# Attention with windows, then soft mixture of experts: the left-over keys in natural order, dispatch weights held still, combine weights divided before use

## The chip, the cores and the metric

The kernel runs on one core of a Trainium2 chip. The metric is the device time of one execution in microseconds. The kernel before took 180.86 us, the median of three runs between 180.55 and 181.25.

A core has a tensor engine (PE, with its weight loads shown as PEld), a vector engine (DVE), a scalar engine (ACT), a general engine (POOL, whose queue starts nearly all transfers here) and a queue for synchronization (SP). Sixteen DMA engines move data between the chip's main memory and the on-chip memory. PE writes into a small accumulator memory (PSUM), from which DVE or ACT copy results out.

## What is computed

Attention runs over 8 batches, 8 heads, 576 positions and 64 channels. The first four heads see a plain window of 32 keys, the last four a dilated one: 32 keys, 4 apart. The result, with heads side by side, is a matrix `x` of 4608 rows and 512 columns, and goes into a soft mixture of 8 experts with 4 slots each:

```
rel = pos[:, None] - pos[None, :]
plain   = (rel >= 0) & (rel < 32)                      # heads 0 to 3
dilated = (rel >= 0) & (rel < 128) & (rel % 4 == 0)    # heads 4 to 7
x = softmax(mask(q k^T / 8)) v                         # 4608 x 512
logits = x @ phi                                       # 4608 x 32 slots
d = softmax of logits over the 4608 rows               # dispatch
slot_input = d^T @ x                                   # 32 x 512
h = relu(slot_input[e] @ w1[e]); slot_out[e] = h @ w2[e]   # F = 1024
c = softmax of logits over the 32 slots                # combine
out = c @ slot_out                                     # 4608 x 512, fp32
```

Inputs are fp32: q, k and v of 9.4 MB each, `w1` and `w2` of 16.8 MB each. The output has 9.4 MB.

## The kernel before

**Transfers.** POOL's queue loads everything but a small table of constants, and converts fp32 to fp16 on the way in and fp16 to fp32 on the way out. It runs in the order of the program. For each batch it loads q, k and v in two parts each (`load_raw`, line 191) into double-buffered tiles, as soon as the tile before has been read. From the fourth batch on, one expert's `w1` follows each v. The rest of `w1` and `w2` follow the last v. The `w2` of experts 5, 6 and 7 come as column halves (line 211): first all first halves, then all second halves. A transfer takes one of eight completion slots, so each waits for the one eight places earlier.

**Attention.** A list of step names (`ORDER`, line 48) fixes by hand the order in which every engine gets its work; each name carries a stage from 0 to 3, so that four batches are in the air at once. In a batch:

- DVE turns q, k and v (`turn`, line 222).
- PE makes scores for groups of key blocks (`emit_scores`, line 263): "P" are five plain blocks of 128 keys, "D" the four dilated residue classes of the first 512 positions, and "L" the last 64 positions of the dilated heads.
- ACT takes the exponentials (line 272), DVE multiplies by 0/1 masks (line 283).
- PE transposes value rows into `vX`, which ACT copies (`v_rows`, `v_place`, lines 237 and 243). Each value row carries an added 1, so that the product also gives the softmax sum.
- PE multiplies probabilities by values (`emit_av`, line 313); DVE takes reciprocals of the sums (line 325); ACT or DVE scale the result into `xp` (plain) or `xd` (dilated) (lines 337 and 341).

For "L", the before kernel handles the 64 left queries by residue class: one score block for the 64 last keys, in which the queries are sorted by class, and 16 more query columns in each "D" block. The product with values is then made in 32 small pieces, each with 16 or 32 rows of result.

**Slots.** For each batch PE transposes x, forms logits (`back_logits`), and ACT takes their exponentials into `ET` (line 408), which stays in memory for all batches with the slots along partitions. `back_erow` and `back_erd` make versions with the rows along partitions. `back_u` (line 451) sums `d^T x` without division: there x is the operand that is held still in PE, and `ET`'s 32 columns stream, in 25 products per batch, 5 of them with a block of ones for the sums. DVE adds the batch's part to `UT` (line 461).

**The end.** After the last batch, PE sums `ET` over slots into `rs` (lines 585 and 590). DVE takes the reciprocals `rcol` (line 593) and `rrow` (line 607), and scales the slot inputs (line 599). PE multiplies by `w1` (`hps`, line 616), ACT and DVE apply the ReLU (lines 623 and 624), PE transposes (line 626), DVE and ACT copy (lines 628 and 631), and PE multiplies by `w2` (`so`, line 646), in two column halves. Four partial sums on partition groups are joined: copied to `so_part` (line 660), added by a product with `spread` (line 665), and copied to `so_sb` (line 666). Then for each block of 128 output rows PE multiplies `ET` by `so_sb` (line 672), and ACT or DVE in turn scale by `rrow` while copying to `om` (lines 681 and 685). POOL's queue stores it (line 692): six batches by column halves, two whole, and the left rows (line 721).

Of the kernel before, what the change touches and what calls it, by code (L numbers as in the profile page):

```python
# [32 lines left out]
NV = 10  # L33
# [3 lines left out]
DW = 144  # L37
LEFT = SUB - 128
# [6 lines left out]
    (("P", 3), ("P", 4), ("L", 0), ("D", 0)),  # L45
# [12 lines left out]
WIDTH = {"P": PW, "L": DIL * LEFT, "D": DW}  # L58


def piece_w(kind, i):
    return S - 512 if (kind, i) == ("P", 4) else WIDTH[kind]

# [15 lines left out]
def make_consts():  # L79

    a = np.arange(128)[:, None]
    rel = np.arange(PW)[None, :] - a
    band = (rel >= 0) & (rel < WINDOW)
    one = np.ones((1, N_SLOTS), bool)
    r, i = np.divmod(np.arange(DIL * LEFT)[None, :], LEFT)
    parts = [band, (a < 64) & (a % DIL == r) & (a // DIL <= i)]
    parts.append(((a % 32) < LEFT) & one)
    parts.append((a < 64) & one)
    parts.append(a == np.arange(128)[None, :])
    parts.append((a % 32) == (np.arange(128)[None, :] % 32))  # L90
    parts.append((a // 32) == np.arange(4)[None, :])
    return np.ascontiguousarray(np.concatenate(parts, axis=1).astype(np.float16))
# [3 lines left out]
def kernel(  # L96
# [18 lines left out]
    band, lmask = cst[:, 0:PW], cst[:, PW : PW + DIL * LEFT]  # L115
    o_em = PW + DIL * LEFT
    o = o_em + 2 * N_SLOTS
    ident = cst[:, o : o + 128]
    spread = cst[:, o + 128 : o + 256]
    quad = cst[:, o + 256 : o + 260]  # L120
    masks = consts.tile([128, NMASK], FP16, name="masks")
    emask = consts.tile([128, 6, N_SLOTS], FP16, name="emask")
    phi_raw = consts.tile([128, 4, N_SLOTS], FP16, name="phi_raw")
    phi4 = consts.tile([128, 4, 4, N_SLOTS], FP16, name="phi4")
    ones = consts.tile([128, 128], FP16, name="ones")
    ET = consts.tile([128, 192 * B], FP16, name="ET")
    UT = consts.tile([128, 5, N_SLOTS], FP32, name="UT")
    rcol = consts.tile([128, N_SLOTS], FP32, name="rcol")
    siTm = consts.tile([128, 4, E_EXP, N_SLOTS], FP16, name="siTm")
    rrow = consts.tile([128, NFIN], FP32, name="rrow")  # L130
# [25 lines left out]
    x_pool = tc.alloc_tile_pool(name="xp", bufs=2)  # L156
# [5 lines left out]
    ring = ctx.enter_context(tc.tile_pool(name="ring", bufs=2, space=bass.MemoryType.PSUM))  # L162
# [6 lines left out]
    def build_masks():  # L169
# [8 lines left out]
        for kind, i in GROUPS[1]:  # L178
            w = piece_w(kind, i)
            copies(o, lmask if kind == "L" else band, w, 1)  # L180
            o += w
        nc.scalar.copy(
            out=emask[:, 4:6, :], in_=cst[:, o_em : o_em + 2 * N_SLOTS].rearrange("p (t s) -> p t s", t=2)
        )
# [39 lines left out]
    V_PARTS = ((0, 1, 2), (3, 4), (5, 6, 7), (8, 9))  # L224

    def v_rows(b, part):
        tiles = V_PARTS[part]
        rg = ring.tile([128, len(tiles), 4, 2, 32], FP16, name=f"rv_{b}_{part}", tag="ring")
        for n_t, t in enumerate(tiles):
            for c in range(2):  # L230
# [4 lines left out]
                else:  # L235
                    rows = vT[:, 1, 512:SK, c]
# [10 lines left out]
    def emit_scores(b, g):  # L247
        kb, qb = kT[b % 2], qT[b % 2]
        sps = psum_s.tile([128, 4, 512], FP32, name=f"s_{b}_{g}", tag="s")
        for kind, i in GROUPS[g]:  # L250
            c0, w = PIECE[(kind, i)][1], piece_w(kind, i)
            for tt in range(2):
                for h in range(4):
# [5 lines left out]
                    elif kind == "D":  # L259
                        kk, qq = kt[:, i:512:DIL], qt[:, i:S:DIL]  # L260
                    else:
                        kk, qq = kt[:, 512:SK], qt[:, 512:S].rearrange("p (i r) -> p r i", r=DIL)
# [11 lines left out]
    def emit_mask(b, g):  # L274
# [4 lines left out]
        else:  # L279
            m = masks[:, 0 : GW[0]].rearrange("p (n w) -> p n w", n=3)[:, :, 0:DW]  # L280
            m = m[:, None, :, :].broadcast_to([128, 4, 3, DW])
# [8 lines left out]
    xp_t, xd_t = {}, {}  # L290

    def emit_av(b, kind, i):
        o = psum_o.tile([128, 4, D + 1], FP32, name=f"o_{b}_{kind}{i}", tag="o")
        jobs, vb = [], vX[b % 2]
        for h in range(4):
            if kind == "L":
                for r in range(DIL):
                    p = probs(b, "L", 0, h, LEFT * r, 32)[0:64]
                    jobs.append((slice(32 * r, 32 * r + 32), p, vb[0:64, 9, h, 0 : D + 1], h))
# [3 lines left out]
        for h in range(4):  # L303
# [3 lines left out]
            elif kind == "L":  # L307
                for r in range(DIL):
                    lhs = probs(b, "D", r, h, 128, LEFT)
                    rows = slice(32 * r, 32 * r + LEFT)  # L310
                    jobs.append((rows, lhs, vb[:, NP + r, h, 0 : D + 1], h))
        for n, (rows, lhs, rhs, h) in enumerate(jobs):
# [4 lines left out]
                start=(n == 0 or (kind == "L" and n < DIL)),  # L317
# [10 lines left out]
    def norm_mult(b, kind, i, o, rc, engine):  # L328
        pool, name = (xp_t, "xp") if kind == "P" else (xd_t, "xd")
        if b not in pool:  # L330
            pool[b] = x_pool.tile([128, 5, 4 * D], FP16, name=f"{name}_{b}", tag=name)
        dst = pool[b][:, 4 if kind == "L" else i, :]
# [18 lines left out]
    def x_half(b, kind, t, c):  # L351
        return (xp_t if kind == "P" else xd_t)[b][:, t, 128 * c : 128 * c + 128]
# [7 lines left out]
    def xT_dil(b, c):  # L360
# [3 lines left out]
        nc.tensor.transpose(rg[:, :, 128:160], x_half(b, "D", DIL, c), ident)  # L364
# [45 lines left out]
    def back_erow(b):  # L410
        m, l = et_cols(b)
        ep = ring.tile([128, 6, N_SLOTS], FP16, name=f"ep_{b}", tag="ring")
        left = ET[0:32, l : l + 128]
# [3 lines left out]
        nc.tensor.transpose(ep[:, 5, :], left, ident[0:32, 0:32])  # L417
        for r in range(DIL):
            nc.tensor.transpose(
                ep[32 * r : 32 * r + 32, 4, :],  # L420
                left.rearrange("p (i r) -> p r i", r=DIL)[:, r, :],
                ident[0:32, 0:32],
            )
        return ep

    def back_er(b, ep):
        er = s_pool.tile([128, 6, N_SLOTS], FP16, name=f"er_{b}", tag="er")
        nc.vector.tensor_tensor(out=er, in0=ep, in1=emask, op=ALU.mult)
# [8 lines left out]
    def back_u(b):  # L437
        up = ring.tile([128, 5, N_SLOTS], FP32, name=f"u_{b}", tag="ring")
        er, erd = er_t.pop(b), erd_t.pop(b)
        jobs = []  # L440
        for t in range(NP):
            e = er[:, t if t < 4 else 5, :]
            for c in range(2):
                jobs.append((c, x_half(b, "P", t, c), e))
            jobs.append((4, ones, e))
        for r in range(DIL + 1):
            e = erd[:, r, :] if r < DIL else er[:, 4, :]
            for c in range(2):
                jobs.append((2 + c, x_half(b, "D", r, c), e))
# [310 lines left out]
```

## Time and profile before

| what | value |
|---|---|
| median of the runs | 180.86 us |
| the profiled execution | 180.9 us, of which 178.9 us are its span |
| busy: PE, DVE, ACT, POOL | 128.0, 125.7, 122.2, 56.2 us |
| PE instructions: products, and weight loads | 2316, 2316 |
| read from main memory, written | 62.07 MB, 9.44 MB |

The span is the time from the first to the last instruction on the core. The profile has a row of forty slices of the span, with the DMA engines' mean share and the data rate of each; groups of equal instructions with their summed busy time and mean duration; timelines; and for each stretch of time the busy time of each engine, the clock granted to PE, the DMA share and the rate. The rate counts bytes as written, so an fp32 load into fp16 is read at twice the rate shown.

### The profile page before, as it was taken

To read this page: it belongs to the slowest core of one execution; us is meant where nothing else is said; L and a number is where in the kernel's file an instruction comes from. 1 tells how busy PE (TensorE), PEld (TensorE's weight loads), DVE (VectorE), ACT (ScalarE), POOL (GpSimd) and SP (SyncE) were. 2 spreads that over 40 slices of the span, in tenths; PEclk is the share of its full clock that TensorE was granted. 3 is DMA by queue.
4 is the path that set the end of the run, shared out by engine and by line. 5 is a ranking of instruction groups with operands and counts; after the bars stand their busy time and mean duration, and the time that the engine had idled before them with its cause. 6 is when DMAs were issued, how large, how long until landed. Compare 5 with 4: busy or idle time off the path is not lost.

```text
span 178.9 us, 5405 instructions
## 1 busy us (share of the span) xinstructions
PE 128.0 (72%) x2316; PEld 84.7 (47%) x2316; DVE 125.7 (70%) x274; ACT 122.2 (68%) x267; POOL 56.2 (31%) x94
## 2 busy tenths in 40 slices
PE   0026838989999999989989999988695346688100
PEld 0014525676667767657767757856434112221000
DVE  6483999999999999999999995472402016789200
ACT  6007757999999999999999999966002016698100
POOL 7544244224224223243420041111112414376400
PEclk9999999999999879999999999687669955555555
DMA  5999999999999999999999999999999999999994
GB/s 91 203 213 208 214 212 210 214 212 216 214 212 213 215 212 215 214 212 216 210 214 215 212 218 220 215 216 220 211 212 191 197 196 219 390 319 397 406 413 135
DMA packets 21448, 40.88 MB, mean 229 GB/s; under 512 B 1713, under 2 KB 14129, under 8 KB 20785
## 3 DMA queue, kind: packets, MB, share of 16 engines
q0 software_dynamic: 21280, 40.41, 114.2%
q8 instruction: 18, 0.29, 0.6%
q1 hardware_dynamic: 144, 0.14, 0.3%
q14 instruction: 6, 0.04, 0.1%
HBM read 62.07 MB, written 9.44 MB: 400 GB/s over the span
## 4 chain that ended last, share of the span: by engine, by line
DMA 52%; DVE 16%; PE 11%; ACT 9%; issue 3%; POOL 2%; POOLq 0%; DVEq 0%
DMA w<-in_moe_w_dram 36%; DMA rawV<-in_v_dram 10%; DMA rawK<-in_k_dram 6%; DVE vT L222 5%; DVE qk L222 4%; DVE p L283 3%; PE f L672 3%; ACT p L272 3%; ACT om L681 2%; PE s L263 2%; PE o_P L313 2%; PE rv L237 2%; ACT xp L337 1%; PE rp L357 1%; ACT vX L243 1%
## 5 line engine op out<-in xcount | busy, mean ns | idle before, releaser
L272 ACT ACTIVATE p<-s 128x1728 f16<-128x1728 f32 (+1 forms) x24 | 42.0, 1749 | 10.7 <-PE s L263 10.6
L263 PE MATMUL s<-qk 32*128 32x144 f16 (+2 forms) x640 | 29.2, 325 | 16.1 <-DVE qk L222 12.3
L313 PEld LDWEIGHTS <-p 128*128 128x128 f16 (+3 forms) x672 | 23.9, 101 | 14.0 <-issue 3.6
L263 PEld LDWEIGHTS <-qk 32*128 32x128 f16 x640 | 17.0, 118 | 20.4 <-DVE qk L222 12.3
L337 ACT ACTIVATE xp<-o_P,rc_P 128x64 f16<-128x64 f32 x96 | 23.8, 384 | 2.4 <-DVE rc_P L325 2.3
L283 DVE TENSOR_TENSOR p<-p,masks 128x1728 f16<-128x1728 f16 (+1 forms) x24 | 25.4, 1082 | 0.0
L243 ACT COPY vX<-rv 128x512 f16<-128x512 f16 (+1 forms) x32 | 23.5, 786 | 1.7 <-PE rv L237 1.6
L313 PE MATMUL o_P<-vX,p 128*128 128x65 f16 (+1 forms) x288 | 20.7, 210 | 1.3 <-DVE xp L341 0.3
L222 DVE STREAM_TRANSPOSE qk<-rawQ 128x576 uint32<-128x576 uint32 x16 | 18.9, 1243 | 2.7 <-DMA rawQ<-in_q_dram 2.7
L222 DVE STREAM_TRANSPOSE qk<-rawK 128x576 uint32<-128x576 uint32 x16 | 19.7, 1241 | 0.5 <-DMA rawK<-in_k_dram 0.5
L222 DVE STREAM_TRANSPOSE vT<-rawV 128x576 uint32<-128x576 uint32 x16 | 19.6, 1238 | 0.4 <-DMA rawV<-in_v_dram 0.4
L237 PE MATMUL rv<-cst,vT 128*128 128x128 f16 x160 | 17.3, 248 | 3.0 <-DVE vT L222 1.7
L211 POOL DMA_DIRECT2D w<-in_moe_w_dram x12 | 8.9, 745 | 29.1 <-DMA w<-in_moe_w_dram 24.8
L685 DVE TENSOR_SCALAR om<-f,rrow 128x256 f16<-128x256 f32 (+1 forms) x28 | 13.5, 518 | 3.9 <-PE f L672 3.1
L237 PEld LDWEIGHTS <-vT 128*128 128x128 f16 x160 | 12.0, 127 | 8.6 <-issue 4.3
L191 POOL DMA_DIRECT2D rawQ<-in_q_dram x16 | 8.9, 557 | 21.5 <-DVE rc_P L325 16.3
L681 ACT ACTIVATE om<-f,rrow 128x256 f16<-128x256 f32 (+1 forms) x28 | 12.8, 503 | 3.3 <-PE f L672 2.6
L672 PE MATMUL f<-so_sb,ET 32*128 32x256 f16 (+1 forms) x60 | 12.1, 420 | 3.7 <-ACT om L681 2.4
L692 POOL DMA_DIRECT2D out_dram<-om x14 | 10.4, 747 | 12.1 <-DVE om L685 9.4
L191 POOL DMA_DIRECT2D rawK<-in_k_dram x16 | 8.7, 548 | 17.1 <-DVE rc_P L325 14.6
L191 POOL DMA_DIRECT2D rawV<-in_v_dram x16 | 8.7, 547 | 10.8 <-DVE rc_P L325 8.0
L372 ACT COPY xT<-rp 128x576 f16<-128x576 f16 x16 | 10.5, 776 | 1.2 <-PE rp L357 1.2
(84 smaller groups left out, 197.4 us busy)
## 6 DMA issues: line engine op xcount, KB each, us to landing
w<-in_moe_w_dram POOLq DMA_DIRECT2D x13, 1024.0 KB, 21.7
out_dram<-om POOLq DMA_DIRECT2D x12, 512.0 KB, 6.2
rawQ<-in_q_dram POOLq DMA_DIRECT2D x16, 288.0 KB, 10.7
rawK<-in_k_dram POOLq DMA_DIRECT2D x16, 288.0 KB, 10.4
rawV<-in_v_dram POOLq DMA_DIRECT2D x16, 288.0 KB, 10.2
w<-in_moe_w_dram POOLq DMA_DIRECT2D x12, 256.0 KB, 16.4
out_dram<-om POOLq DMA_DIRECT2D x2, 1024.0 KB, 8.6
out_dram<-om_l POOLq DMA_DIRECT2D x2, 512.0 KB, 9.1
```

The costliest lines, as they stand in the source:

```text
L191: nc.gpsimd.dma_start(out=t[g::2, :], in_=src[4 * g : 4 * g + 4].rearrange("h (p j) d -> (h p) (j d)", j=PJ),)
L222: nc.vector.transpose(out=out_, in_=in_)
L237: nc.tensor.transpose(rg[:, n_t, :, c, :], rows, ident)
L243: copy(out=vX[b % 2][:, t0 : t0 + n, :, 0:D], in_=rg.rearrange("p n h c d -> p n h (c d)"))
L263: nc.tensor.matmul(sps[:, h, c0 : c0 + w], kk, qq, start=(tt == 0), stop=(tt == 1))
L272: return nc.scalar.activation(out=pt, in_=sps[:, :, 0:n], func=AF.Exp, scale=SCALE)
L283: return nc.vector.tensor_tensor(out=pt, in0=pt, in1=m, op=ALU.mult)
L313: nc.tensor.matmul(o[rows, h, :], lhs, rhs, start=(n == 0 or (kind == "L" and n < DIL)), stop=(n == len(jobs) - 1), skip_group_check=True,)
L337: nc.scalar.activation(out=dst[:, h], in_=src[:, h], func=AF.Copy, scale=rc[:, h : h + 1])
L672: nc.tensor.matmul(fp[:, 0 : c1 - c0], ET[32 * j : 32 * j + 32, m : m + 128], so_sb[32 * j : 32 * j + 32, c0:c1], start=True, stop=True,)
L681: nc.scalar.activation(out=dst, in_=fp[:, 0 : c1 - c0], func=AF.Copy, scale=rrow[:, blk : blk + 1])
L685: nc.vector.tensor_scalar(out=dst, in0=fp[:, 0 : c1 - c0], scalar1=rrow[:, blk : blk + 1], scalar2=None, op0=ALU.mult)
```

## The change

Four things change.

1. The 64 left queries of the dilated heads stay in natural order. There are now two "L" score blocks, each with 128 neighbouring keys, from 448 and from 384 on, with a mask of their own; the "D" blocks lose their 16 extra columns. The product with values takes two products of 128 keys for each head instead of eight small ones. A value tile is added (11 instead of 10).
2. In `back_u` the row version of `ET` is held still and x streams, with a column of ones stored beside x. The 25 products become 10, and the sum has the slots along partitions. At the end it is scaled, transposed back by PE and copied into `siTm`.
3. The combine weights are divided in place: for each pair of batches PE sums `ET` over the slots with a block matrix, DVE takes the reciprocal of 128x384 elements and multiplies. Two such divisions stand before the products with `w1`, two between their halves. `rrow` disappears.
4. Output blocks are copied two at a time, without scaling, by ACT and DVE in turn. The first products with `w2` take 512 columns, and the joins of `so` are made in one copy per half, the second one wholly before the sixth batch's output.

```
-NV = 10
+NV = 11
-DW = 144
-LEFT = SUB - 128
+LEFT = S - 512
+XW = 4 * D + 2
...
-    (("P", 3), ("P", 4), ("L", 0), ("D", 0)),
+    (("P", 3), ("P", 4), ("L", 0), ("L", 1), ("D", 0)),
...
+LKEY = (448, 384)
...
-    V_PARTS = ((0, 1, 2), (3, 4), (5, 6, 7), (8, 9))
+    V_PARTS = ((0, 1, 2), (3, 4), (5, 6, 7), (8, 9, 10))
...
                     elif kind == "D":
-                        kk, qq = kt[:, i:512:DIL], qt[:, i:S:DIL]
+                        kk, qq = kt[:, i:512:DIL], qt[:, i:512:DIL]
                     else:
-                        kk, qq = kt[:, 512:SK], qt[:, 512:S].rearrange("p (i r) -> p r i", r=DIL)
+                        kk, qq = kt[:, LKEY[i] : LKEY[i] + 128], qt[:, 512:S]
...
             if kind == "L":
-                for r in range(DIL):
-                    p = probs(b, "L", 0, h, LEFT * r, 32)[0:64]
-                    jobs.append((slice(32 * r, 32 * r + 32), p, vb[0:64, 9, h, 0 : D + 1], h))
+                for n in range(2):
+                    lhs = probs(b, "L", n, h, 0, 128)
+                    jobs.append((slice(0, 128), lhs, vb[:, NP + DIL + n, h, 0 : D + 1], h))
...
     def back_u(b):
-        up = ring.tile([128, 5, N_SLOTS], FP32, name=f"u_{b}", tag="ring")
+        up = ring.tile([64, 4 * D + 1], FP32, name=f"u_{b}", tag="ring")
         er, erd = er_t.pop(b), erd_t.pop(b)
...
+            n = LEFT if t == 4 else 128
+            for k, x in enumerate((xp_t[b % 2], xd_t[b % 2])):
+                e = erd[:, t, :] if k == 1 and t < 4 else er[0:n, t, :]
+                nc.tensor.matmul(
+                    up[32 * k : 32 * k + 32, :],
+                    e,
+                    x[0:n, t, 0 : 4 * D + 1],
+                    start=(t == 0),
+                    stop=(t == NP - 1),
+                )
...
+    nc.vector.reciprocal(out=rcol, in_=U[:, 4 * D : 4 * D + 1])
+    nc.vector.tensor_scalar(out=si, in0=U[:, 0 : 4 * D], scalar1=rcol, scalar2=None, op0=ALU.mult)
+    siT = ring.tile([128, 2, 2, N_SLOTS], FP16, name="siT", tag="ring")
+    for c in range(2):
+        nc.tensor.transpose(
+            siT[:, c].rearrange("p k s -> p (k s)"), si[:, 128 * c : 128 * c + 128], ident[0:64, 0:64]
+        )
...
+    def normalize(pr):
+        cols = ET[:, 384 * pr : 384 * pr + 384]
+        rs = ring.tile([128, 384], FP32, name=f"rs_{pr}", tag="ring")
+        rr = h_pool.tile([128, 384], FP32, name=f"rr_{pr}", tag=f"rr{pr % 2}")
+        nc.tensor.matmul(rs, block, cols, start=True, stop=True)
+        nc.vector.reciprocal(out=rr, in_=rs)
+        nc.vector.tensor_tensor(out=cols, in0=cols, in1=rr, op=ALU.mult)
+
+    for pr in range(2):
+        normalize(pr)
...
     for fc in range(2):
+        if fc == 1:
+            for pr in range(2, 4):
+                normalize(pr)
         for g in range(2):
...
+    psum_f = tc.alloc_tile_pool(name="psum_f", bufs=3, space=bass.MemoryType.PSUM)
...
+    def join_so(s):
+        cols = slice(DH * s, DH * s + DH)
+        nc.vector.tensor_copy(out=so_part[:, cols], in_=so[:, cols])
+        nc.tensor.matmul(rep[:, cols], spread, so_part[:, cols], start=True, stop=True)
+        nc.scalar.copy(out=so_sb[:, cols], in_=rep[:, cols])
+
+    def emit_fin(blocks, c0, c1, dst, name, copy):
+        fp = psum_f.tile([128, 2, DMODEL], FP32, name=f"f_{name}_{c0}", tag="f")
+        for n, (m, j) in enumerate(blocks):
...
+        copy(out=dst, in_=fp[:, :, 0 : c1 - c0])
...
+    EVICT = (nc.scalar.copy, nc.vector.tensor_copy)
...
-    for s in range(2):
-        emit_so(s, (0, 1, 2, 3))
-    for s in range(2):
-        emit_so(s, (4,))
+    emit_so(None, (0, 1, 2, 3))
+    emit_so(None, (4,))
     for e in (5, 6, 7):
         emit_so(0, (e,))
-    gather_so(0)
-    spread_so(0)
+    join_so(0)
     for b in range(NHALF):
         if b in (2, 3, 5):
             emit_so(1, ({2: 5, 3: 6, 5: 7}[b],))
         if b == 5:
-            gather_so(1)
+            join_so(1)
         emit_batch(b, 0, DH)
-    spread_so(1)
```

## The prediction

> **What bounds the kernel now.** I read the page first, then the table of stretches over the end, the timelines of VectorE, ScalarE and the POOL queue, and last the groups with shapes kept apart. From the page:
>
> ```profile
> span 178.9 us, 5405 instructions
> ...
> DMA  5999999999999999999999999999999999999994
> GB/s 91 203 213 208 214 212 210 214 212 216 214 212 213 215 212 215 214 212 216 210 214 215 212 218 220 215 216 220 211 212 191 197 196 219 390 319 397 406 413 135
> ...
> q8 instruction: 18, 0.29, 0.6%
> ```
>
> The DMA engines never rest: fp32 inputs come in at some 213 GB/s of fp16 written (twice that read), and the fp32 result leaves at 400. VectorE, ScalarE and TensorE are busy too, but only the transfers are busy from end to end. So compute matters where it decides when a transfer can start, and that is at one place: the first output store. From the table of stretches (after the stretch: busy time and count of PE, PEld, DVE, ACT, POOL, then PE clock, DMA share, GB/s):
>
> ```profile
> 146.00:150.00 4.00, 2.69 (x26) 0.94 (x22) 2.33 (x6) 2.21 (x6) 0.69 (x1) 0.50 1.45 195
> 150.00:151.00 1.00, 0.45 (x12) 0.14 (x8) 0.88 (x2) 0.84 (x2) 0.81 (x2) 0.50 1.22 186
> ...
> 157.00:159.00 2.00, 1.71 (x9) 0.48 (x9) 1.55 (x4) 1.83 (x5) 1.39 (x2) 0.50 1.08 214
> 159.00:176.00 17.00, 6.16 (x23) 1.14 (x20) 7.24 (x13) 6.33 (x12) 6.57 (x10) 0.50 1.73 401
> ```
>
> The stores replace the last loads almost without a hole (only 150 to 151 and 157 to 159 sag). From the POOL timeline, the last load and the first and sixth store:
>
> ```profile
> 143.36 0.74 POOL L211 DMA_DIRECT2D w<-in_moe_w_dram  x1 [1.44 <-DMA w<-in_moe_w_dram]
> ...
> 149.31 0.75 POOL L692 DMA_DIRECT2D out_dram<-om  x1 [5.21 <-DVE om L685]
> ...
> 157.61 2.96 POOL L692 DMA_DIRECT2D out_dram<-om  x4 [2.73 <-DVE om L685]
> ```
>
> Each transfer marks its landing 16 times in the trace, once per DMA engine. The last load's marks run from 150.10 to 153.58 us, so the engines are up to 3.5 us apart. The trace's 18 instruction packets (16 KB each, 18 for PE's 4632 instructions, one per 257) explain this: half of the 16 marks trail, and after the packets at 22.1, 80.6 and 140.7 us the latest mark falls 0.7 to 0.9 us further back. The latest engine has three. It is busy from 153.58 to the last mark, 177.39; the span ends 1.5 us later. Sixth store to last, 12 half-batches take 15.5 us between first marks: 1.29 us each. A store reaching idle engines lands 3.0 us after its issue (149.31 to 152.31, 157.61 to 160.62), so its data start after 1.7.
>
> Two rates for the change, from the timelines of ScalarE and VectorE and the groups:
>
> ```profile
> 95.95 1.61 ACT L243 COPY vX<-rv 128x768 f16<-128x768 f16 x2
> 97.32 1.07 ACT L337 ACTIVATE xd<-o_D,rc_D 128x64 f16<-128x64 f32 x4
> ...
> 98.91 0.79 ACT L243 COPY vX<-rv 128x512 f16<-128x512 f16 x1
> 99.37 1.83 ACT L272 ACTIVATE p<-s 128x1728 f16<-128x1728 f32 x1
> ```
> ```profile
> 79.10 0.16 DVE L325 RECIPROCAL rc_D<-o_D 128x4 f32<-128x4 f32 x1
> 79.14 0.15 DVE L325 RECIPROCAL rc_P<-o_P 128x4 f32<-128x4 f32 x1
> ...
> 127.43 0.32 DVE L461 TENSOR_TENSOR UT<-UT,u 128x160 f32<-128x160 f32 x1 [0.92 <-PE u L451]
> ...
> 128.38 0.37 DVE L607 RECIPROCAL rrow<-rs 128x36 f32<-128x36 f32 x1
> 135.06 0.69 DVE L624 TENSOR_SCALAR h_sb<-hps 128x512 f16<-128x512 f32 x1 [6.30 <-ACT h_sb L623]
> ```
> ```profile
> L685 DVE TENSOR_SCALAR om<-f,rrow 128x256 f16<-128x256 f32 x24 | 10.6, 480 | 3.6 <-PE f L672 3.0
> ...
> L325 DVE RECIPROCAL rc_P<-o_P 128x4 f32<-128x4 f32 x40 | 6.1, 168 | 2.9 <-PE o_P L313 2.6
> ...
> L685 DVE TENSOR_SCALAR om<-f,rrow 128x512 f16<-128x512 f32 x4 | 2.9, 748 | 0.3 <-PE f L672 0.2
> ...
> L607 DVE RECIPROCAL rrow<-rs 128x36 f32<-128x36 f32 x1 | 0.4, 374 | 0.0
> ```
>
> ScalarE runs back to back in the attention: start to start, a 768-wide value copy takes 0.69 us and a 512-wide one 0.46. From 4 to 36 elements a reciprocal grows by (374-168)/32 = 6.4 ns an element, where an eviction of VectorE grows by (748-480)/256 = 1.05.
>
> **The change part by part**, along the chain that leads to the first store. It starts at 127.75, the end of the last UT sum.
>
> A. Attention. The exponentials and masks keep their sum (1920+1920+1536 columns for 1920+1728+1728). TensorE loses some 33 small products a batch net and gains two value transposes; that is worth nothing, because ScalarE sets the pace, and could only cost if TensorE (4.6 of 5 us busy) became the slower one, which less work excludes. The fourth value copy grows from 512 to 768: 0.21 us in each of 8 batches on the engine that never waits, 1.7 us; ScalarE pauses some 0.3 us a batch, and the first batch is not full. I take +1.3 (ends 0 and 1.7). The loads do not notice: POOL keeps 4 to 7 transfers in flight here.
>
> B. Dispatch sums. 25 products of 32 columns (0.82 us for the last batch) become 10 of 257, two at a time on separate output strips. At the half clock four 512-column products of hps (L616) run together: their weight loads come in fours, 0.43 us apart. So a 257-column pair takes 0.21: 5 pairs and a tail, 1.3 us, less four small transposes. With 257 instead of 160 elements to add: +0.45 (ends 0; 1.5 if pairs don't overlap).
>
> C. To the first wide reciprocal: reciprocal 0.17, slot scaling 0.39, two transposes 0.35, the product with `block` 0.45: 1.35 us.
>
> D. The four divisions of `ET` now stand on VectorE ahead of the ReLU of line 624 that today starts at 135.06. Each is a reciprocal of 384 elements, 168+380x6.4 = 2.6 us, and a 384-wide product at about 0.5 (0.40 for 256, row L341): 4x3.1 = 12.4. Ends: at a copy's rate 4x1.07 = 4.3; at the 10 ns an element that the starts 79.10 and 79.14 allow, 4x4.4 = 17.6, though that interval may be a floor for short instructions. I trust the difference of durations. Today's pause of VectorE (6.3 us before L624) hides half of it; the ReLU moves to 143.2. Behind the divisions on VectorE stand that ReLU, the copy of `hT`, and `so_part`, and for these wait TensorE, ScalarE and POOL. On TensorE the last two `block` products wait for buffers of the first two reciprocals and hold up the second half of hps to some 138 us; the divisions are still later, so that is free.
>
> E. ReLU to the first `so` product: 137.03-135.06 = 1.97 us, unchanged.
>
> F. `so`, first half: today its products wait for loads until 145.6. Now all are there, and 10 groups of 512 columns (both halves of experts 0 to 4) and 6 of 256 come in a row: at the half clock, which PE will have after its pause, 10x0.43+6x0.21 = 5.6 us; at full clock 2.8. I take 5.3.
>
> G. `so` to the first store's issue: 149.31-146.04 = 3.3 us. Wider join copies cost 0.1 each, the pairwise eviction (128x512: 0.69 and 0.75 us) gains as much. POOL's list of transfers is the same, and nothing but stores queues behind this wait; SP has the constants alone.
>
> Sum: 127.75+1.3+0.45+1.35+12.4+1.97+5.3+3.3 = 153.8 us, 4.5 later than now. From an idle start the span ends 1.7+18x1.29+0.3+1.5 = 26.7 us after the first issue: 180.5, against 178.9. The break-even is a first issue at 152.2.
>
> Later on nothing adds: evictions at 0.75 us a half-batch, POOL's issue (0.75) and the join of the second half (some 1.5 us, with four stores queued) keep up with 1.29. The reserved gain is hidden: PE's 4010 instructions need 15 blocks instead of 18, so no engine has three; that is worth 0.7 to 0.8 us only if the stores are ready when the loads end. Constants (32 KB more), memsets and smaller copies lie beside the first loads, cost 0 to 0.1.
>
> The profiled execution took 180.9 us, 2.0 beyond its span, and the median of the runs is 180.86. So 180.9+1.6 = 182.5 us.
>
> [...]
>
> **Rivals.**
> 1. Reciprocals cost midway between durations and start-to-start interval, 8.2 ns an element: 3.3 us each, D is 15.4, the time 185.5. For it speaks 79.10 to 79.14; against it the durations. [...]
> 2. Not slower: the wide reciprocal streams better than short ones. If D falls to 4.3, the first store could go at 145.7; the loads then decide, and the missing third block gives 180.9-0.8 = 180.1. Below D = 10.8 us the change costs nothing, below 9.8 the loads decide. Against it: nothing in the trace shows a reciprocal at that rate.
> 3. In between: D as said, but `so` at full clock (-2.5) or no delay from A (-1.3): first issue 151.3 to 152.5, time 180.1 to 181.2. For it: hps brought the clock up 4.4 us after its start at 128.5.
> 4. The change doesn't reduce what bounds: certain for the products, since ScalarE paces attention and DMA the whole.
>
> **How the numbers follow.** A measurement here tells 0.5%, 0.9 us. Forecast (181.8 to 184.0, own range) 0.46; rival 1 and longer 0.14; rivals 2 and 3 in the band 180.0 to 181.7, 0.27; below it 0.13, where rival 2 meets a further lost stall, such as the 157 to 159 sag. So 0.13 faster, 0.27 same, 0.60 slower. The range reaches from the floor of rival 2 to rival 1: 180.0 to 185.3.
>
> **What would show it.** Wide reciprocals of 2.6 us; the ReLU near 143; the first store near 153.8 with DMA share falling towards zero between 151 and 155; 15 instruction packets; no landing spread of 3.5 us. I am wrong if the ReLU starts before 140, or if the stores have further holes.

## The result and the profile after

The changed kernel takes 182.14 us (median of 22 runs, 180.68 to 183.93), the kernel before 181.04 us (22 runs beside them, 180.55 to 181.66). The ratio is 1.0053, with a 95% interval from 1.0038 to 1.0069: slower by half a per cent. A run more than 1.5% above the fastest of its kernel (183.93 here, and one such run below) stays out of the ratios. The profiled execution took 182.9 us, 1.8 more than its span; for the kernel before the distance was 2.0.

From the page of the changed kernel:

```profile
span 181.1 us, 4758 instructions
...
DMA  5999999999999999999999999999999997999997
GB/s 112 172 205 210 211 212 213 213 213 216 210 213 214 215 213 214 211 214 213 212 214 215 213 215 223 217 213 212 221 203 193 196 196 101 271 394 399 402 412 208
...
q8 instruction: 15, 0.25, 0.5%
```

There are 15 instruction packets where there were 18. Slice 34 sags to 101 GB/s, and the first two slices are at 112 and 172 GB/s, before at 91 and 203. The table of stretches shows the hole (the columns are those of the table of before: busy time of PE, PEld, DVE, ACT, POOL, then PE clock, DMA share, GB/s):

```profile
146.00:150.00 4.00, 3.48 (x38) 1.31 (x40) 0.42 (x1) 0.58 (x1) 0.00 (x0) 0.54 1.45 196
150.00:151.00 1.00, 1.00 (x36) 0.61 (x24) 0.00 (x0) 0.00 (x0) 0.00 (x0) 1.00 1.13 161
151.00:153.50 2.50, 0.90 (x17) 0.39 (x9) 1.08 (x2) 1.09 (x3) 0.00 (x0) 1.00 0.56 73
153.50:155.80 2.30, 2.06 (x34) 0.84 (x37) 1.88 (x4) 1.87 (x4) 1.57 (x3) 1.00 0.29 61
155.80:157.00 1.20, 0.38 (x9) 0.10 (x4) 1.06 (x3) 0.18 (x1) 1.20 (x2) 0.80 1.99 404
```

For almost five microseconds the transfers have next to nothing to do: from 151.0 to 155.8 the rate is 73 and then 61 GB/s, while `so`, which TensorE ended at 151.15, is joined and the first output blocks are made. Stores run only from 155.8. VectorE, the groups with shapes kept apart, and the POOL timeline say why:

```profile
130.31 0.41 DVE L443 TENSOR_TENSOR U<-U,u 64x257 f32<-64x257 f32 x1 [1.33 <-PE u L429]
...
132.11 2.56 DVE L583 RECIPROCAL rr<-rs 128x384 f32<-128x384 f32 x1 [0.24 <-PE rs L582]
134.70 0.56 DVE L584 TENSOR_TENSOR ET<-ET,rr 128x384 f16<-128x384 f16 x1
...
143.88 0.56 DVE L584 TENSOR_TENSOR ET<-ET,rr 128x384 f16<-128x384 f16 x1
144.36 0.68 DVE L608 TENSOR_SCALAR h_sb<-hps 128x512 f16<-128x512 f32 x1
146.21 0.42 DVE L612 COPY hTm<-hT 128x512 f16<-128x512 f16 x1 [1.17 <-PE hT L610]
```
```profile
L583 DVE RECIPROCAL rr<-rs 128x384 f32<-128x384 f32 x4 | 10.2, 2552 | 0.2 <-PE rs L582 0.2
...
L584 DVE TENSOR_TENSOR ET<-ET,rr 128x384 f16<-128x384 f16 x4 | 2.2, 558 | 0.1
```
```profile
154.10 3.84 POOL L671 DMA_DIRECT2D out_dram<-om  x5 [10.25 <-ACT om L658]
160.71 2.96 POOL L671 DMA_DIRECT2D out_dram<-om  x4 [2.77 <-DVE om L658]
```

The four divisions fill VectorE from 132.11 to 144.36 without a pause, the ReLU stands behind them, and POOL waits 10.25 us for the first block of output, where it waited 5.21. The first store goes at 154.10 instead of 149.31.

Not all of this is the divisions. The attention also starts later, as the first exponential shows, in the kernel before and then in the changed one:

```profile
13.30 1.77 ACT L272 ACTIVATE p<-s 128x1920 f16<-128x1920 f32 x1 [8.95 <-PE s L263]
```
```profile
14.96 1.77 ACT L270 ACTIVATE p<-s 128x1920 f16<-128x1920 f32 x1 [10.48 <-PE s L261]
```

### The profile page after: what moved, and what is told of

Same layout as the page of the kernel before. It is cut to its first block, busy times and chain, and to the rows that moved or that the text cites. A ratio compares the mean times of both kernels' runs of the same rounds, so it can differ in the third digit from the quotient of the medians.

```text
span 181.1 us, 4758 instructions
## 1 busy us (share of the span) xinstructions
PE 119.3 (66%) x2004; PEld 78.3 (43%) x2004; DVE 134.3 (74%) x267; ACT 119.0 (66%) x251; POOL 56.2 (31%) x94
## 4 chain that ended last, share of the span: by engine, by line
DVE 47%; DMA 15%; PE 11%; ACT 11%; issue 5%; POOL 1%; DVEq 1%; POOLq 0%; ACTq 0%
DVE qk L219 12%; DVE p L281 8%; DVE vT L219 8%; DMA rawV<-in_v_dram 6%; DVE rr L583 6%; DMA phi_raw<-in_moe_phi_dram 6%; DMA rawK<-in_k_dram 4%; DVE xd L329 4%; PE so L633 3%; PE f L651 2%; ACT p L270 2%; DVE om L658 2%; ACT xp L325 2%; ACT om L658 2%; ACT xT L366 2%
## 5 line engine op out<-in xcount | busy, mean ns | idle before, releaser
L270 ACT ACTIVATE p<-s 128x1920 f16<-128x1920 f32 (+1 forms) x24 | 44.3, 1847 | 12.1 <-PE s L261 11.9
L261 PE MATMUL s<-qk 32*128 32x128 f16 (+2 forms) x704 | 26.7, 295 | 20.2 <-DVE qk L219 13.9
L241 ACT COPY vX<-rv 128x768 f16<-128x768 f16 (+1 forms) x32 | 27.5, 932 | 1.9 <-PE rv L235 1.9
L304 PEld LDWEIGHTS <-p 128*128 128x128 f16 (+1 forms) x480 | 22.1, 102 | 13.5 <-issue 4.0
L325 ACT ACTIVATE xp<-o_P,rc_P 128x64 f16<-128x64 f32 x96 | 26.3, 490 | 2.2 <-DVE rc_P L316 2.2
L281 DVE TENSOR_TENSOR p<-p,masks 128x1920 f16<-128x1920 f16 (+1 forms) x24 | 25.6, 1082 | 0.1
L235 PEld LDWEIGHTS <-vT 128*128 128x128 f16 x176 | 13.1, 124 | 7.8 <-issue 3.8
L671 POOL DMA_DIRECT2D out_dram<-om x14 | 10.3, 745 | 13.1 <-ACT om L658 10.2
L658 DVE CAST om<-f 128x512 f16<-128x512 f32 (+1 forms) x14 | 10.2, 765 | 3.7 <-PE f L651 3.7
L304 PE MATMUL o_D<-vX,p 128*128 128x65 f16 x128 | 9.9, 202 | 2.3 <-DVE xp L329 1.7
L366 ACT COPY xT<-rd 128x576 f16<-128x576 f16 x16 | 10.6, 790 | 0.2 <-PE rd L352 0.2
```

The source lines that it names most:

```text
L235: nc.tensor.transpose(rg[:, n_t, :, c, :], rows, ident)
L241: copy(out=vX[b % 2][:, t0 : t0 + n, :, 0:D], in_=rg.rearrange("p n h c d -> p n h (c d)"))
L261: nc.tensor.matmul(sps[:, h, c0 : c0 + w], kk, qq, start=(tt == 0), stop=(tt == 1))
L270: return nc.scalar.activation(out=pt, in_=sps[:, :, 0:n], func=AF.Exp, scale=SCALE)
L281: return nc.vector.tensor_tensor(out=pt, in0=pt, in1=m, op=ALU.mult)
L304: nc.tensor.matmul(o[rows, h, :], lhs, rhs, start=(n == 0), stop=(n == len(jobs) - 1), skip_group_check=True,)
```

## The experiments

First the price of the divisions by itself, then its break-even, the parts that pay for some of it, and two causes that fell. What a profile gives of each kernel is gathered at the end of this section.

**Two divisions moved.** The first two divisions stay; the third goes behind the copy of `hT`, the fourth into the second half of the stores.

```
     for pr in range(2):
-        normalize(pr)
+        divide(pr, ring_sums(pr))
     ...
         if fc == 1:
-            for pr in range(2, 4):
-                normalize(pr)
+            rs_2 = ring_sums(2)
     ...
+    divide(2, rs_2)
     ...
         emit_batch(b, DH, DMODEL)
+        if b == 2:
     ...
+            divide(3, sums(3, f3[:, 0, 0:384]))
```

Here `normalize` is split in two: `sums` and `ring_sums` are its product on TensorE, `divide` its reciprocal and product on VectorE.

> The changed kernel with the four divisions kept but two of them moved: the third stands behind the copy of hT, the fourth behind the third half-batch of the second half (nine stores out). Chain theory (the end is the first store's issue plus 27 us as soon as that issue is later than about 152.2; the four divisions, 12.3 us on VectorE ahead of the ReLU, make it late): the ReLU starts about 138.5 instead of 144.4, the first store goes at 148.5 to 150.5, the loads decide again, time 180.0 to 180.6 us, below the kernel before. Rival 'late start' (in the profile of the changed kernel one DMA engine runs 2.3 us behind from the first loads on and the first exponential starts 1.66 us later; that is what costs, the divisions cost nothing net): 182 us, as the changed kernel. Rival 'stores' (the pairwise evictions and the joins make the store phase longer): 182 us too, with 27 us or more after the first store.

Measured: 180.07 us (179.84 to 180.74), ratio to the kernel before 0.9949 (0.9934 to 0.9964). From its VectorE and POOL timelines:

```profile
129.44 2.56 DVE L585 RECIPROCAL rr<-rs 128x384 f32<-128x384 f32 x1
...
136.04 0.69 DVE L612 TENSOR_SCALAR h_sb<-hps 128x512 f16<-128x512 f32 x1 [0.40 <-ACT h_sb L611]
137.54 0.42 DVE L616 COPY hTm<-hT 128x512 f16<-128x512 f16 x1 [0.80 <-PE hT L614]
137.88 2.55 DVE L585 RECIPROCAL rr<-rs 128x384 f32<-128x384 f32 x1
140.46 0.56 DVE L586 TENSOR_TENSOR ET<-ET,rr 128x384 f16<-128x384 f16 x1
145.65 0.42 DVE L649 CAST so_part<-so 128x256 f16<-128x256 f32 x1 [4.63 <-PE so L638]
```
```profile
148.66 0.75 POOL L676 DMA_DIRECT2D out_dram<-om  x1 [5.04 <-ACT om L663]
```

The same reciprocals, the same 2.55 us each, but the ReLU now ends a wait of 0.40 us (put down to ScalarE's half of the ReLU) and not a queue of divisions, and the third division lies in VectorE's wait for `so`, which still leaves 4.63 us. The ReLU starts at 136.04, 2.5 us ahead of the expectation; the first store at 148.66 and the time are inside it. The chain theory holds. The edit leaves the code of the start and of the pairwise evictions as it was, so neither rival expects the gain. This execution did start earlier than the profiled one of the changed kernel (first exponential 13.77 for 14.96); that an early start alone does not make the kernel fast is shown by two runs below, with every reciprocal twice (13.46) and with the divisions in the kernel before (13.22).

**No divisions.**

```
-    for pr in range(2):
-        normalize(pr)
     ...
-            for pr in range(2, 4):
-                normalize(pr)
```

> The changed kernel with the division of the combine weights left out (the sums, the reciprocals and the products; the output is then not divided). Chain theory: the ReLU starts at 137 to 138 (hps decides), loads decide, 180.0 to 180.6 us, the same as with two divisions moved. Late start or stores: 182 us.

Measured: 180.11 us (180.01 to 180.85), ratio 0.9956 (0.9939 to 0.9973). Leaving the divisions out gains no more than moving two of them. The ReLU starts at 136.31, a little ahead of the expectation. At this end the loads decide: the time is the last load's latest mark, 153.91, plus 26.9 us.

**Every reciprocal twice.**

```
         nc.vector.reciprocal(out=rr, in_=rs)
+        nc.vector.reciprocal(out=rr, in_=rs)
```

> The changed kernel with each of the four wide reciprocals issued twice, 4 x 2.55 = 10.2 us more on VectorE. Chain theory: all of it reaches the end, since the first store is already later than the loads: first store 164.3, time 192.3 (191.8 to 192.8). If the divisions were partly hidden in the changed kernel (late start or stores decide), less than 10.2 arrives, by as much as was hidden: 188 to 191.

Measured: 191.12 us (190.24 to 193.54, four runs), ratio 1.0539 (1.0504 to 1.0574), so some 9 of the 10.2 us arrive. The median lies between the ranges of the two; by the ratio the time is 190.8 us, inside that of the rival. The timeline has all the extra time (130.97 to the ReLU at 153.59, 22.6 us where the changed kernel has 12.25, and a first store at 164.30, as expected), but its execution is the one of 193.54 us; the other three took 190.24, 190.28 and 191.95. Why a microsecond or more is missing in them isn't settled.

**One division moved**, the fourth alone:

```
-            rs_2 = ring_sums(2)
+            divide(2, ring_sums(2))
     ...
-    divide(2, rs_2)
```

> The changed kernel with the fourth division alone moved behind nine stores, the other three left ahead of the ReLU: 3.1 us off the chain. Chain theory with its break-even at a first store of 152.2 (so that D costs nothing below 10.8 us and the loads decide below 9.8): D is 9.2 us, first store 150.2 to 151.2, time 180.1 to 180.5 us, all but as good as two divisions moved (180.07). Rival (no sharp break-even, since the 16 DMA engines end their loads 3 us apart, so each us of the chain costs part of itself on the early ones): about halfway between 180.07 and 182.14, 180.8 to 181.3.

Measured: 180.16 us (179.77 to 180.51), ratio 0.9960 (0.9941 to 0.9979). Taking 3.1 us off the chain gains all that there is, 2.0; the further 3.1 of the first experiment gain nothing that can be told from zero. The break-even of the prediction is there, and the rival's gradual price is not. How sharp it is isn't shown: the first store of the profiled execution went before the expected 150.2 to 151.2, some 2 us ahead of the break-even.

```profile
149.28 2.37 POOL L675 DMA_DIRECT2D out_dram<-om  x3 [6.17 <-ACT om L662]
```

**The left block's products five times over**, on top of two divisions moved:

```
-        for n, (rows, lhs, rhs, h) in enumerate(jobs):
+        for _ in range(5 if kind == "L" else 1):
+            for n, (rows, lhs, rhs, h) in enumerate(jobs):
```

> Two divisions moved, and the products of the left block issued five times over (each repetition starts its sums anew, the result is the same): 512 more instructions on TensorE, 4522, so 17 or 18 instruction packets of 16 KB again instead of 15, the 17th before the last loads land as in the kernel before. ScalarE still sets the pace of the attention (the kernel before has more instructions). Packet theory (a third packet on one DMA engine puts it 0.7 to 0.9 us further back, and the latest engine ends the kernel): 180.7 to 181.0 us. Rival (what is gained against the kernel before comes from the evictions in pairs, the joins or what lies outside the span): 180.0 to 180.2 us, as without the repetitions.

Measured: 180.76 us (180.33 to 181.05), ratio 0.9985 (0.9971 to 0.9999), where it was 0.9949 without the repetitions: 0.7 us more. The page has the packets:

```profile
span 179.1 us, 5271 instructions
...
q8 instruction: 17, 0.28, 0.6%
```

In this trace the last load's latest mark falls at 153.89, in the one without repetitions at 153.31, and the first store still goes in time (149.99). The last mark alone would not tell, since the kernel without divisions has one at 153.91 with 15 packets, after a start that was later on one engine. But the step itself can be seen. Here and without repetitions the eighth load's marks spread over 0.97 and 0.99 us, and the last load's first mark falls at 150.17 and 150.14. Only the latest mark moves: around the 17th packet, at 147.9, the spread goes from 3.07 us in one load to 3.94 in the next, where the kernel without repetitions stays at 3.15 to 3.17. So the packet theory stands: with the packets back, most of the gain against the kernel before is gone. About a quarter of a microsecond more of that gain lies outside the span (1.76 us here and with two divisions moved, 2.0 in the kernel before); what it is isn't shown.

One part of the expectation fell: ScalarE does not go on setting the pace. The 32 extra products in each batch, with their weight loads, made a batch of the attention 0.7 us longer (13.58 for 12.86) and the whole attention 5.1 us, and from 55 to 80 us ScalarE is busy for 24.39 of 25 us and VectorE for 23.59, where without them they are for 25.00 and 24.92. This reaches the first store only by 1.3 us, and that is still before the break-even. In the traces of the kernel before and of the changed one the instruction packets have 16384 bytes each (18 beside 2316 products of TensorE and as many weight loads, 15 beside 2004). Here 512 instructions more for TensorE, in 17 packets, cost 0.7 us.

**The divisions in the kernel before**, and nothing else of the change:

```
     nc.vector.reciprocal(out=rrow, in_=rs)
+    nc.tensor.matmul(ds, spread, ET[:, 0:384], start=True, stop=True)
+    for _ in range(4):
+        nc.vector.reciprocal(out=dr, in_=ds)
+        nc.vector.tensor_tensor(out=dt, in0=ET[:, 0:384], in1=dr, op=ALU.mult)
```

> The kernel before with four dummy divisions (reciprocal and product of 128 x 384, result unused) on VectorE where the change has them, and nothing else of the change. Chain theory: VectorE's pause of 6.3 us hides half of the 12.3, the ReLU goes from 135.06 to 141.2, the first half of so then runs in a row on loads that are there, first store 149.5 to 152, break-even 152.2: time 181.0 to 181.6 us. Rival (the division alone explains the changed kernel's time): 182.1 us.

Measured: 183.37 us (181.77 to 184.33), ratio 1.0123 (1.0076 to 1.0169), above both expectations. Its VectorE timeline:

```profile
129.27 0.32 DVE L461 TENSOR_TENSOR UT<-UT,u 128x160 f32<-128x160 f32 x1 [0.91 <-PE u L451]
...
130.52 2.50 DVE L613 RECIPROCAL dr<-ds 128x384 f32<-128x384 f32 x1
...
143.08 0.68 DVE L631 TENSOR_SCALAR h_sb<-hps 128x512 f16<-128x512 f32 x1
```

The divisions take what they should (12.6 us). But the last dispatch sum ends at 129.60, where the profile that the prediction was made from has 127.75: the attention of this execution was longer, from the first exponential to the last transposition of `ET` 114.3 us against 112.4. So the base was 1.85 us too early for this execution, and the first store goes at 153.31, after the expected 149.5 to 152. From there to the end it takes 30.2 us, where the changed kernel takes 28.8. And the divisions alone cost more than the whole change: its other parts give back about 1.2 us, though the four runs lie 2.6 us apart. The difference behind the first store would account for it. One place where the stores differ is the stretch from 160 to 162 us, here and then in the changed kernel:

```profile
160.00:162.00 2.00, 1.71 (x9) 0.40 (x7) 1.56 (x4) 1.83 (x5) 1.50 (x3) 0.50 1.39 278
```
```profile
160.00:162.00 2.00, 1.62 (x12) 0.56 (x12) 1.67 (x4) 1.66 (x3) 1.29 (x2) 0.50 1.97 391
```

Which of the other parts (the evictions in pairs, the joins) does it, no run separates.

**A shorter value copy.** In the changed kernel, step A undone:

```
-        copy(out=vX[b % 2][:, t0 : t0 + n, :, 0:D], in_=rg.rearrange("p n h c d -> p n h (c d)"))
+        n = min(n, NV - 1 - t0)
+        copy(out=vX[b % 2][:, t0 : t0 + n, :, 0:D], in_=rg[:, 0:n].rearrange("p n h c d -> p n h (c d)"))
     ...
+        nc.vector.memset(vX[i][:, NV - 1, :, 0:D], 0.0)
```

> The changed kernel with the fourth value copy of ScalarE 512 wide as before, not 768 (the second key tile of the left block is left zero, so the last 64 queries of the dilated half are wrong). Step A of the prediction: 8 x 0.21 us less on the engine that sets the pace, 1.3 us (0 to 1.7) of it on the chain: last dispatch sum 1.3 us earlier, time 180.6 to 181.0 where the changed kernel has 182.1. Rival (the later end of the attention is the late start alone, ScalarE has pauses that hide the copies): 182.

Measured: 181.04 us (180.35 to 182.88, ten runs), ratio 1.0022 (0.9989 to 1.0055). The median says 1.1 us, but the runs fall into two groups with a hole between: six from 180.35 to 181.26 at a mean granted clock of .882 to .884, and four from 182.48 to 182.88 at .848 to .856. The changed kernel's own runs at .882 to .900 are 180.68 to 180.94, and those at .846 to .857 are 182.49 to 183.28. At like clocks the shorter copy is worth some 0.1 to 0.3 us, though the changed kernel's runs between these clocks (.864 to .877) spread from 181.19 to 183.93. Over four batches in the middle of the attention a batch takes 12.87 us here, 12.91 in the changed kernel, 12.86 in the one without divisions and 12.87 in the kernel before. From the tables of stretches, 55 to 80 us, of the kernel before, the changed one, and this one:

```profile
55.00:80.00 25.00, 23.64 (x501) 17.21 (x485) 24.81 (x56) 24.81 (x55) 7.19 (x13) 0.93 1.06 213
```
```profile
55.00:80.00 25.00, 21.55 (x435) 16.06 (x428) 24.93 (x57) 25.00 (x56) 7.96 (x14) 1.00 1.06 213
```
```profile
55.00:80.00 25.00, 22.86 (x442) 16.36 (x439) 24.94 (x56) 24.99 (x57) 7.57 (x14) 1.00 1.06 213
```

VectorE (third number) is as full as ScalarE (fourth), with the long copy and without. ScalarE alone doesn't set this pace. Over the whole attention the copy does show: in three profiles whose granted clock was 0.99 or 1.00 throughout, the attention takes 112.44 and 112.47 us with the long copy (no divisions, two moved) and 111.72 with the short one. That is 0.7 us, from one profile of the short copy.

**The join moved.** On top of two divisions moved, `so` of expert 7 and the join of the second half go behind the sixth half-batch:

```
-        if b in (2, 3, 5):
-            emit_so(1, ({2: 5, 3: 6, 5: 7}[b],))
-        if b == 5:
-            join_so(1)
+        if b in (2, 3):
+            emit_so(1, ({2: 5, 3: 6}[b],))
         emit_batch(b, 0, DH)
+    emit_so(1, (7,))
+    join_so(1)
```

> Two divisions moved, and the so products of expert 7 with the join of the second half moved behind the sixth batch of the first half, so that the sixth store no longer waits for the last load (its issue 158.1 becomes about 154.5). Theory 'latest engine' (the end is the engine whose last load lands at 153.3, plus 18 units of 1.29 us; early engines that run dry around 157 to 160 lose nothing that counts): 179.7 to 180.1 us, at most 0.4 better than 180.07. Rival 'hold' (the slice at 270 instead of 400 GB/s, 1.45 us of transfer, is lost to all): 178.6 us.

Measured: 179.93 us (179.43 to 180.11), ratio 0.9938 (0.9915 to 0.9961). The stretches before and after this edit, two divisions moved first:

```profile
154.00:158.00 4.00, 3.01 (x20) 0.93 (x20) 2.83 (x6) 2.61 (x5) 0.46 (x1) 0.50 1.71 346
158.00:162.00 4.00, 2.00 (x14) 0.63 (x14) 3.97 (x5) 1.76 (x3) 2.96 (x4) 0.50 1.52 310
```
```profile
154.00:158.00 4.00, 2.75 (x18) 0.85 (x18) 2.32 (x4) 2.07 (x5) 2.09 (x4) 0.50 1.92 387
158.00:162.00 4.00, 1.99 (x12) 0.52 (x10) 3.96 (x5) 1.72 (x3) 1.16 (x3) 0.50 1.98 398
```

The sag is gone (346 and 310 GB/s become 387 and 398) and the time hardly moves: 0.14 us, with intervals that overlap. The sixth store goes at 155.83, not 154.5. The rival "hold" falls. That the time stays the last mark plus 26.9 us in both fits the theory that what ran dry there were engines that had been early, and that the latest one ends the kernel.

**The constants.** Three kernels ran beside each other. The version with the join moved, with the small constants of the kernel before:

```
-    parts.append((a // 32) == (np.arange(128)[None, :] // 32))
+    parts.append((a // 32) == np.arange(4)[None, :])
     ...
+    nc.scalar.copy(
+        out=block.rearrange("p (j i) -> p j i", j=4), in_=quad[:, :, None].broadcast_to([128, 4, 32])
+    )
```

> As the version with two divisions and the join moved, but the constants are 548 columns as in the kernel before, not 672: the 128 x 128 block pattern is spread out from 4 columns by one ScalarE copy while ScalarE is idle. In the profiles so far the DMA engine that is furthest behind at the eighth load was 0.57 and 0.60 us behind in two with the small constants, and 0.58 to 2.31 us (mean 1.2) in eight with the large ones; the time of the kernels that loads decide was the last mark of the last load plus 26.9 us in each. Theory 'constants' (the larger transfer at the start puts one engine behind): lag about 0.6, time 0.3 to 0.6 us below the control, 179.3 to 179.6. Rival (the lag differs from execution to execution whatever the constants are): no difference, 179.9.

The control with the large constants:

> Control for the version with the small constants, the same kernel as two divisions and the join moved: 179.9 us, 0.6% below the kernel before, by either theory.

The kernel before with large ones:

```
+    parts.append(np.zeros((128, 124), bool))
```

> The kernel before with 124 columns of zeros behind its constants, 672 columns as in the change, never read. Theory 'constants': lag of the latest engine at the eighth load about 1.2 instead of 0.6, time 0.3 to 0.6 us longer, 181.3 to 181.6. Rival: no difference, 181.0 us.

Measured: 179.65 us (ratio 0.9925, 0.9911 to 0.9938) with the small constants, 179.92 (0.9938, 0.9924 to 0.9952) for the control, and 180.90 (1.0009, 0.9991 to 1.0027) for the kernel before with large ones, which itself took 180.93 here. The theory falls in the kernel before, where nothing changes. In the other pair the intervals overlap; and the trace with the small constants has the latest engine 1.39 us behind at the eighth load, its control 0.94. The kernel before with large ones has 1.01 us there, near the 1.2 of the theory, but its time does not follow. So the constants aren't shown to make the late start. Why it differs from execution to execution stays open.

**What the profiles give together.** Attention is the time from the first exponential to the last transposition of `ET`; clock is the granted clock from 14 to 110 and from 110 to 127 us; last mark is that of the last load, on the latest of the 16 engines.

| kernel | time | first exponential | attention | clock | first store | last mark |
|---|---|---|---|---|---|---|
| before | 180.9 | 13.30 | 112.40 | .98, .77 | 149.31 | 153.58 |
| before, large constants | 181.14 | 13.68 | 116.57 | .86, .75 | 150.13 | 153.80 |
| before, with divisions | 183.48 | 13.22 | 114.32 | .93, .80 | 153.31 | 153.29 |
| changed | 182.9 | 14.96 | 113.35 | .98, .90 | 154.10 | 153.53 |
| short value copy | 181.26 | 14.06 | 111.72 | 1.00, 1.00 | 151.73 | 153.64 |
| no divisions | 180.85 | 14.31 | 112.44 | 1.00, .99 | 149.46 | 153.91 |
| one moved | 179.77 | 13.19 | 113.31 | 1.00, .85 | 149.28 | 152.80 |
| two moved | 180.26 | 13.77 | 112.47 | 1.00, 1.00 | 148.66 | 153.31 |
| two moved, left products five times | 180.82 | 13.71 | 117.61 | 1.00, 1.00 | 149.99 | 153.89 |
| two moved, and the join | 180.0 | 13.80 | 114.43 | .95, .90 | 148.26 | 153.07 |

Where the first store goes before 150.2, the time is the last mark plus 26.9 us, within 0.1 in these kernels and 0.15 in the version with small constants and its control (27.3 in the two kernels with the old evictions). It follows neither the first exponential nor the length of the attention. In the changed kernel it is the first store's issue plus 28.8 instead. With a last mark of 153.3 the two cross at 153.3+26.9-28.8 = 151.4; the prediction had the break-even at 152.2. Near the crossing neither rule is exact: the short value copy has its first store at 151.73 and ends 0.7 us later than both give.

## Why the prediction was right

The forecast was 182.5 us, and slower; it is 182.14, and slower: 1.1 us above the kernel before in the runs beside it, where 1.6 was forecast. Its mechanism (a longer VectorE chain ahead of the ReLU, which makes the first store later than the loads) is shown by the moved divisions, by their absence and by the doubled reciprocals. By its steps, against the profile of the changed kernel:

- **Base and A.** Wrong in both terms, in opposite directions. With B, the last dispatch sum was to end 1.75 us later; it ends 2.97 later. Of this 1.66 is a later first exponential, which no step had: the first loads land on one engine some 2.3 us behind. 0.95 is a longer attention (113.35 for 112.40), and 0.36 is B. The 1.3 us of A, which the step put on ScalarE because it "never waits", are too many. The copy grows by the 0.2 us it was given, but a batch in the middle stays at 12.9 us: four dilated evictions take 0.07 us less of ScalarE's time, some pause was left to fill, and VectorE is as full. At a full granted clock the long copy costs the attention 0.7 us (112.44 and 112.47 for 111.72). The rest of what lengthens the attention goes along with the clock, which is argued below and not shown.
- **B** was 0.45, measured 0.36. **C** was 1.35, measured 1.39.
- **D.** 12.4 forecast, 12.25 measured: 4 x 2.552 and four products of 0.558, overlapping by some 0.05 at each step. The slope of 6.4 ns an element, taken from groups of 4 and 36 elements, held at 384: (2552-374)/(384-36) = 6.3. With it rival 1 falls, which had 8.2.
- **E** was 1.97, measured 2.33: the eight transposes of `hT` took 1.07 us, not 0.71, at a granted clock of 0.50, after PE had stood idle for 5.16 us; in the kernel before the clock was 1.00 there, after 1.49 us.
- **F** was 5.3, measured 4.46. The clock came up part of the way through (0.54 from 146 to 150, 1.00 from 150 on). **G** was 3.3, measured 2.95.
- The sum came out at 154.10 for 153.8 because a late start and a longer attention (2.6) stand where A (1.3) was put, and F and G were 1.2 too long. That the total agrees to 0.3 us is partly luck. So is the time: the profiled execution is 0.8 us slower than the median, for which 182.14-28.8 puts the first store near 153.3 by estimate, and 2.0 us were taken for what lies outside the span, which is 1.8 here.
- **From the first store to the end**: 27.0 for 26.7.
- **The packets**: 15, as said. But the landing spread of the last load hardly shrank: from 3.47 to 3.14 us, with the late start in place of the third packet. Once all engines had run dry, the first store's marks lay within 0.35 us, so in this kernel the gain was gone.
- **Rival 2** gave 180.1 us if D cost nothing. With divisions moved or left out it is 180.07 to 180.16. The 0.8 us that it put on the missing packets compares with the 0.7 that the packets cost when they come back. **Rival 3** has the times of the three single runs at the highest clocks (180.68 to 180.94); they have no trace, so whether by its reasons isn't shown. **Rival 4** holds in that the products taken from TensorE bought nothing at the end of this kernel. Its reason, that ScalarE alone paces the attention, does not hold: VectorE is as full, and 32 products more in each batch made the attention 5.1 us longer.

## What to carry to other kernels

Before adding work to an engine that has long pauses, ask which of those pauses lie on the chain to the next transfer; here four divisions ahead of the ReLU cost 2 us, and nothing that can be told from zero once one or two of them stand behind it. Where transfers bound a kernel, look at the latest of the DMA engines, not at their mean: filling a sag in the mean gained some 0.1 us, and giving TensorE 512 instructions more cost 0.7. The version with two divisions and the join moved and the small constants takes 179.65 us, 0.75% below the kernel before (0.62 to 0.89%).

## What the runs showed of the hardware that was not expected

The granted clock of TensorE falls to 0.73 inside the attention on this one core, while TensorE is busy for 24.15 of 25 us. The kernel before with large constants, table of stretches:

```profile
55.00:80.00 25.00, 24.15 (x478) 18.65 (x475) 23.37 (x52) 23.77 (x55) 7.16 (x13) 0.73 1.06 213
80.00:105.00 25.00, 23.91 (x464) 18.05 (x461) 23.39 (x53) 24.11 (x51) 5.78 (x10) 0.73 1.06 214
```

At 0.73 TensorE (first number) is the fullest engine, VectorE and ScalarE have pauses, and the attention takes 116.57 us instead of 112.40. This execution took 181.14 us all the same, as its loads decide (last mark 153.80, plus 27.3). Over the runs of the kernel before beside the three groups of experiments time and mean clock hardly go together in two (correlations of +0.19 over 17 runs and -0.06 over 23) and somewhat in the third (-0.58 over 17, on another chip); over the 23, at clocks of .781 to .862, the times lie between 180.46 and 181.94. In the kernels whose chain decides it shows more: the correlation is -0.62 over the 22 runs of the changed kernel and -0.97 over the ten of the short value copy, which lie in two clusters. The changed kernel scatters over 3.3 us, the versions with one or two divisions moved over 0.7 to 0.9. No run set the clock by itself, so that it is the cause is argued from these rows and not shown. Nor is it shown what lowers it: the version with 512 more instructions for TensorE ran at the highest clocks, .889 to .905.
